# Moving the score visits of an attention and mixer kernel to a schedule that repeats with the batch

## The chip, the cores and the metric

The kernel runs on one core of one Trainium2 chip. A core has five engines that run their own instruction streams: TensorE (PE) for matrix products, VectorE (DVE), ScalarE (ACT), GpSimd (POOL) and SyncE (SP); the last two mostly issue DMAs here. Matrix products go to PSUM, which the program uses as eight banks, and VectorE or ScalarE carry the results from there to SBUF. The metric is the device time of one execution in microseconds, the median of several runs.

## The reference

Eight batches, eight heads, 576 tokens, head width 64. Attention with a causal mask over the tokens, in front of which 16 beacon keys and values stand that every token sees:

```python
k_all = np.concatenate([beacon_k, k], axis=2)
v_all = np.concatenate([beacon_v, v], axis=2)
scores = scale * np.matmul(q, k_all.transpose(0, 1, 3, 2))
causal[:, Nb:] = np.triu(np.ones((S, S), dtype=bool), k=1)
scores = np.where(causal, -1000000000.0, scores)
a = np.exp(scores - scores.max(-1, keepdims=True))
a /= a.sum(-1, keepdims=True) + 1e-09
x = np.matmul(a, v_all)              # heads side by side: (8, 576, 512)
```

Then a mixer: a low-rank product along the tokens (rank 32) with a residual, and two layers of width 2048 with a residual:

```python
h = x.transpose(0, 2, 1) @ U @ V
u = x + h.transpose(0, 2, 1)
out = u + np.maximum(u @ w_ch1, 0.0) @ w_ch2
```

## The kernel before, in words

**Attention in pairs.** The work goes by pairs of heads, p = 0 to 31, four pairs a batch. The score matrix of a pair (keys down, queries across, the causal half only) is cut into four groups of columns, 0 to 3, 496, 464, 496 and 208 wide; each group takes one PSUM bank for each of the two heads. `visit(parts)` (L370) computes the scores of some groups: it takes all its banks, issues the matmuls (L379) for both heads in turn, and then one exponential a bank on ScalarE (L385), which writes to one of four tiles `expt`. `masks_of(p)` (L722) lets VectorE put the masked entries of both heads to zero (L321, L323). `av_of(p)` (L725) gives two units, one a head: 15 matmuls (L394) of the weights with the values, then a reciprocal and a multiply on VectorE (L402, L403) that write into `xb`, the batch's attention output x.

**The mixer.** `mix_units` (L415) gives four steps for a batch once x is there. `turn` (L420) issues five DMA transposes on SP's queue, which write x turned into `uT`. `head` (L426) multiplies x with U: 20 small matmuls and a copy on VectorE. `most` (L449) multiplies with V: it takes four banks, one matmul each (L456), and VectorE adds each to `uT` (L443). `end` (L463) does the last 80 tokens in one bank (L469, L443). 

**The layers.** `mlp_units` (L515) cuts each block of 512 tokens into 32 layer units of four 512-wide matmuls: 16 of the first layer (L531, each with a bank and an eviction into `gT` by ScalarE, L544, or VectorE, L546) and 16 of the second, four to a bank (L557); after the fourth VectorE adds the residual (L570) and SP writes the block out (L576). They stand in `queue`; `fill(n)` issues the next n of them between other work. All orders on all engines are written by hand: the program's order is the order of each engine's stream.

**Banks.** `pst` (L105) takes the bank that was given back longest ago, and `emptying` gives one back in program order when its eviction is issued. So a matmul into a bank waits for the eviction of whatever had it before, and how far back that lies is set by the order of the program alone.

**The stage of the change.** From pair 16 on (`P6`, batches 4 to 7), keys and queries come ready turned by DMA (`turns`, L647: ten transposes a batch on SP's queue, issued at the start of the batch before), and scores are computed in visits of three groups, six banks. 15 pairs with four groups make 20 visits. `long_slot` (L953) is one pair's slot, and its form goes by `r = (p - P6) % 3`: in three slots four visits, whose groups cross from one pair to the next. A batch has four slots, so the visits fall elsewhere in each batch. `mix_between` (L928) runs in a batch's last slot, after the second value product: it issues `turn`, and leaves `head`, `most` and `end` in `mixing`. `head` follows the next visit of a slot with r = 0. `between_visits` (L948) issues `most` at the first call by which at least eight layer units (`SINCE`) have gone by, and puts `end` into the queue three places on, where it counts as a unit. Pairs 16 to 31 have queue places for 131 units, four of which hold an `end`.

Of the kernel before, what the change touches and what calls it, by code (L numbers as in the profile page):

```python
# [30 lines left out]
def kernel(  # L31
# [21 lines left out]
    NH2 = H // 2  # L53
# [51 lines left out]
    def pst(shape, dtype, name):  # L105

        b = emptied.pop(0)
        t = psum.tile(shape, dtype, tag=f"bank{b}", name=name)
        bank_of[id(t)] = (b, t)
        return t  # L110

    def emptying(t):
        emptied.append(bank_of.pop(id(t))[0])
# [256 lines left out]
    def visit(parts):  # L370

        at = {p: (p % NH2, qTs[p // NH2], kTs[p // NH2 % 2], expts_of(p)) for p, _ in parts}
        ps = {(p, g, i): pst([P, 512], F32, name=f"sps{i}") for p, g in parts for i in range(2)}
        for p, g in parts:
            c, qT, kT, _ = at[p]
            for ch, qa, w, o in groups[g]:
                for i in range(2):
                    hp = slice(D * i, D * i + D)
                    nc.tensor.matmul(  # L379
                        ps[p, g, i][:, ds(o, w)], kT[hp, c, ds(P * ch, P)], qT[hp, c, ds(qa, w)],  # L380
                        start=True, stop=True,
                    )
        for p, g in parts:
            for i in range(2):
                nc.scalar.activation(  # L385
                    out=at[p][3][i][:, ds(SLOT * g, gw[g])], in_=ps[p, g, i][:, 0 : gw[g]], func=AF.Exp, scale=scale
                )
                emptying(ps[p, g, i])

    def av_unit(b, h, ex, vs, xb):  # L390
        po = pst([P, NT, E], F32, name="po")
        for j in range(NT):
            for c in range(j + 1):
                nc.tensor.matmul(  # L394
                    po[:, j, :],
                    ex[0 : nk[c], ds(blk[(c, j)], P)],
                    vs[0 : nk[c], ds(c * H * E + h * E, E)],
                    start=(c == 0),
                    stop=(c == j),
                )  # L400
        r = rec[:, b * H + h, :, :]
        nc.vector.reciprocal(out=r, in_=po[:, :, D : D + 1])  # L402
        nc.vector.tensor_tensor(  # L403
            out=xb[:, :, ds(h * D, D)], in0=po[:, :, 0:D], in1=r.broadcast_to([P, NT, D]), op=ALU.mult
        )
        emptying(po)
# [216 lines left out]
    NP = B * NH2  # L623
# [3 lines left out]
    def load_batch(b):  # L627
        if b < DT0:
            Ls[b] = qk_tiles()
            emit_loads(b, Ls[b], vss[b % 2])  # L630
        else:
            v_loads(v[b], beacon_v[b], vss[b % 2])

    def load_whole(b):

        Ls[b] = qk_tiles()
        for i, (src, m) in enumerate(((k[b], nk), (q[b], nq))):
            dst = Ls[b][1][i]
            if i == 0:
                beacon_load(nc.gpsimd, beacon_k[b], dst[:, 0, :, :], ALLH)  # L640
            for j in range(NT):
                a = m[j] - nq[j]
                nc.gpsimd.dma_start(  # L643
                    out=dst[a : m[j], j, :, :], in_=src[:, ds(q0[j], nq[j]), :].rearrange("h p d -> p h d")
                )
# [39 lines left out]
    def regroup_of(p):  # L685
        b, c = divmod(p, NH2)
        prs[p] = [regroup(Ls[b][0], c, i, nc.vector.tensor_copy) for i in range(2)]
# [27 lines left out]
    def expts_of(p):  # L715
        return [expts[(2 * p + i) % NE] for i in range(2)]

    def scores_of(p):
        b, c = divmod(p, NH2)
        return score_units(c, qTs[b], kTs[b % 2], expts_of(p), p < NM)  # L720

    def masks_of(p):  # L722
        scores_of(p)[2]()

    def av_of(p):  # L725
        b, c = divmod(p, NH2)
        if c == 0:
            xbs[b] = xbp.tile([P, NT, DM], F16, name="xb", tag="xb")
        return [
            lambda i=i: av_unit(b, 2 * c + i, expts[(2 * p + i) % NE], vss[b % 2], xbs[b]) for i in range(2)  # L730
        ]
# [5 lines left out]

    DT0 = 4
    LAG = 10
    SINCE = 8  # L740
    HINT = 5

    FIRST = [3, 3, 2, 1]
# [4 lines left out]
    queue = []  # L748
    state = {"t": 0}

    def fill_turns(tr, n):
        for u in tr[:n]:
            u()
        del tr[:n]

    def fill(n):
        while n > 0 and queue:
            u = queue.pop(0)
            if u is not None:
                u()  # L760
            n -= 1

    def feed(b):

        while state["t"] < NBLK and 512 * (state["t"] + 1) <= S * (b + 1):
            t = state["t"]
            units, state["part"] = mlp_units(
                512 * t, 512, lambda i, m, t=t: rows[ds(512 * t + P * i, m), :], t % 2, t > 0, t == NBLK - 1
            )
            queue.extend(units)  # L770
            state["t"] += 1
# [18 lines left out]
    with tc.manual_schedule(engines={ENG.PE, ENG.Activation, ENG.DVE, ENG.SP, ENG.Pool}):  # L790
# [42 lines left out]
        for p in range(2):  # L833
# [4 lines left out]
            av = av_of(p)  # L838
# [5 lines left out]
        av = av_of(2)  # L844
# [8 lines left out]
        av = av_of(3)  # L853
# [30 lines left out]
        for p in range(NH2, NP1):  # L884
            b, c = divmod(p, NH2)
# [39 lines left out]
        P6 = DT0 * NH2  # L925
        mixing = []

        def mix_between(b):  # L928

            turn, head, parts = mix_units(xbs[b], S * b)  # L930
            turn()
            mixing[:] = [head] + parts
            state["since"] = 0
            feed(b)

        def go(n):
            fill(n)
            state["since"] += n

        def visit_then_head(parts):  # L940
            parts = [(p, g) for p, g in parts if p < NP]
            if not parts:
                return
            visit(parts)
            if len(mixing) == 3:
                mixing.pop(0)()

        def between_visits():  # L948
            if len(mixing) == 2 and state["since"] >= SINCE:
                mixing.pop(0)()  # L950
                queue.insert(3, mixing.pop(0))

        def long_slot(p, av):  # L953

            r = (p - P6) % 3
            if r == 0:
                visit_then_head([(p + 1, 0), (p + 1, 1), (p + 1, 2)])
            go(2)
            if r and p < NP:
                masks_of(p)  # L960
            between_visits()
            go(3 if r == 2 else 2)
            av[0]()
            go(1)
            av[1]()
            if p % NH2 == NH2 - 1 and p + 1 < NP:
                mix_between(p // NH2)
            go(1)
            if r == 0:
                visit_then_head([(p + 1, 3), (p + 2, 0), (p + 2, 1)])  # L970
            elif r == 1:
                visit_then_head([(p + 1, 2), (p + 1, 3), (p + 2, 0)])
            else:
                visit_then_head([(p + 1, 1), (p + 1, 2), (p + 1, 3)])
                go(2)
                between_visits()
                go(2)
                if p + 1 < NP:
                    masks_of(p + 1)
                go(2)  # L980

        for p in range(NP1, NP):
            b, c = divmod(p, NH2)
            if c == (1 if p >= P6 else 0) and b + 1 < B:
                load_batch(b + 1)
            if c == 2 and DT0 <= b + 2 < B:
                load_whole(b + 2)
            if c == 0 and b + 1 == DT0:
                tr = turns(b + 1)
            if c == 0 and DT0 < b + 1 < B:  # L990
                tr = turns(b + 1)
            sc = scores_of(p + 1) if p < P6 else []
            qk = qkT_of(p + 2) if p + 2 < min(NP, DT0 * NH2) else []
            av = av_of(p) if p < P6 else []
            if c == 0 and b + 1 == DT0:
                fill_turns(tr, NT)
            if c == 0 and b > NF and p <= P6:
                (mix if p < P6 else mix_between)(b - 1)
            if c == 1 and b + 1 == DT0:
                fill_turns(tr, NT)  # L1000
            if c == 0 and b + 1 > DT0:
                fill_turns(tr, 2 * NT)
            if p >= P6:
                long_slot(p, av_of(p))
                continue
            seq = sc[0:1] + av[0:1] + qk[0:1] + sc[1:3] + qk[1:2] + av[1:2]
            if p + 3 < min(NP, DT0 * NH2):
                seq.append(lambda p=p: regroup_of(p + 3))
            quota = QUOTA.get(b, 9)
            done = 0  # L1010
            for i, u in enumerate(seq):
                u()
                want = quota * (i + 1) // len(seq)
                fill(want - done)
                done = want
# [59 lines left out]
    with tc.If(n_bad != 0, label="general"):  # L1075
        with tc.For_i(0, B, 1) as bi:
# [10 lines left out]
            _, head, parts = mix_units(xb, 0, False)  # L1087
# [3 lines left out]
            for t0 in range(0, S, 512):  # L1091
                n = min(512, S - t0)
# [32 lines left out]
```

## Time and profile before

| What | Value |
|---|---|
| Time of three runs, median | 359.1 us (358.96 to 359.97) |
| Profiled execution, its own time | 360.71 us |
| Profiled execution, span from first to last instruction | 359.1 us |
| Granted TensorE clock in that execution, mean | 0.999 |
| Stage with six-bank visits (first and last L379) | 131.8 to 269.3 us |
| Score matmuls of that stage (L379) | 180 |
| Products with the values in all (L394) | 960 |

In the lines of the profile, PE is TensorE's matmuls and PEld its weight loads, DVE VectorE, ACT ScalarE, SP and POOL the two that issue DMAs; a q behind the name is the engine's queue. L379 is line 379 of the program. A line of a timeline gives start, duration, engine, source line, operation, what is written and from what, the shape, and how many alike were put together; in brackets the idle time of the engine before it and what ended it. A matmul's duration runs from its issue to its end, and the next one streams meanwhile.

### The profile page before, as it was taken

What the parts mean: (1) busy time and instruction counts of PE and PEld (TensorE: products, weight loads), DVE (VectorE), ACT (ScalarE), POOL (GpSimd) and SP (SyncE); (2) the same over time, 40 slices, a digit from 0 to 9 for tenths busy, and PEclk for the clock granted to TensorE, in tenths of its full rate; (3) what the DMA queues carried; (4) which work ended last, traced back from release to release, by engine and by line L of the source; (5) the groups of instructions that cost most, each with busy time, mean ns of one, the idle gap of its engine ahead of it and who ended that gap; (6) DMA issues with size and microseconds to landing.
All of it is one profiled execution on the core that took longest, in us unless ns stands there. A gap on an engine that the chain in (4) does not pass through costs nothing.

```text
span 359.1 us, 7837 instructions
## 1 busy us (share of the span) xinstructions
PE 349.5 (97%) x3110; PEld 176.1 (49%) x3110; DVE 187.3 (52%) x484; ACT 165.5 (46%) x359; POOL 97.7 (27%) x137
## 2 busy tenths in 40 slices
PE   8999999999999999899999999999999999999995
PEld 3774555455554444445444444454544544444443
DVE  4665874588967644652563545544644634313311
ACT  4976951487733664338523663277225202301400
POOL 8956705327446047202840220000000000000000
PEclk9999999999999999999999999999999999999999
DMA  9999999999999949996999797333013323013111
GB/s 179 97 206 167 154 204 174 210 154 131 103 162 148 172 33 124 149 211 71 133 138 197 118 111 127 108 92 64 32 60 88 58 69 102 16 58 93 26 60 65
DMA packets 146636, 41.89 MB, mean 117 GB/s; under 512 B 131488, under 2 KB 142080, under 8 KB 146592
## 3 DMA queue, kind: packets, MB, share of 16 engines
q0 software_dynamic: 87440, 18.18, 66.2%
q1 hardware_dynamic: 58928, 22.84, 36.3%
q8 instruction: 26, 0.43, 0.5%
q10 hardware_dynamic: 224, 0.30, 0.3%
q14 instruction: 18, 0.15, 0.2%
HBM read 37.37 MB, written 9.44 MB: 130 GB/s over the span
## 4 chain that ended last, share of the span: by engine, by line
PE 82%; DMA 7%; DVE 5%; SPq 2%; ACT 1%; issue 1%; DVEq 0%
PE gps L531 32%; PE cps L557 29%; PE po L394 7%; DMA uT<-xb 5%; PE sps L345 4%; SPq L422 2%; PE sps L379 2%; DVE uT L443 2%; PE tps L274 2%; DMA kT<-st 1%; PE tps L280 1%; PE cph L583 1%; ACT expt L351 1%; DMA stq<-in_q_dram 1%; DVE xb L403 1%
## 5 line engine op out<-in xcount | busy, mean ns | idle before, releaser
L531 PE MATMUL gps<-uT,w 128*128 128x512 f16 x576 | 135.2, 380 | 0.1
L557 PE MATMUL cps<-w,gT 128*128 128x512 f16 x560 | 130.8, 380 | 0.3 <-DVE xb L403 0.3
L544 ACT ACTIVATE gT<-gps 128x512 f16<-128x512 f32 x86 | 52.1, 614 | 83.8 <-PE gps L531 81.9
L557 PEld LDWEIGHTS <-gT 128*128 128x128 f16 x560 | 50.8, 98 | 60.6 <-issue 5.4
L531 PEld LDWEIGHTS <-w 128*128 128x128 f16 x576 | 52.0, 98 | 57.9 <-issue 2.1
L385 ACT ACTIVATE expt<-sps 128x496 f16<-128x496 f32 (+2 forms) x120 | 51.5, 535 | 52.0 <-PE sps L379 52.0
L351 ACT ACTIVATE expt<-sps 128x496 f16<-128x496 f32 (+2 forms) x136 | 58.8, 556 | 21.6 <-PE sps L345 21.5
L546 DVE TENSOR_SCALAR gT<-gps 128x512 f16<-128x512 f32 x58 | 39.9, 690 | 47.6 <-PE gps L531 46.6
L570 DVE TENSOR_TENSOR ob<-cps,ut 128x512 f32<-128x512 f32 x31 | 21.4, 690 | 47.0 <-PE cps L557 46.5
L217 POOL DMA_DIRECT2D vs<-in_v_dram x50 | 39.8, 810 | 18.4 <-DMA st<-in_beacon_k_dram 5.2
L394 PEld LDWEIGHTS <-expt 128*128 128x128 f16 (+1 forms) x960 | 36.1, 98 | 14.5 <-issue 2.2
L394 PE MATMUL po<-vs,expt 128*128 128x65 f16 (+1 forms) x960 | 39.4, 194 | 0.3 <-DVE expt L321 0.3
L403 DVE TENSOR_TENSOR xb<-po,rec 128x320 f16<-128x320 f32 x64 | 31.5, 491 | 2.2
L402 DVE RECIPROCAL rec<-po 128x5 f32<-128x5 f32 x64 | 12.0, 188 | 27.8 <-PE po L394 27.7
L321 DVE TENSOR_TENSOR expt<-expt,bigmask 128x512 f16<-128x512 f16 x54 | 22.5, 416 | 5.8 <-ACT expt L385 3.4
L199 POOL DMA_DIRECT2D vs<-in_beacon_v_dram x8 | 4.3, 540 | 63.8 <-PE po L394 63.7
L443 DVE TENSOR_TENSOR uT<-ups,uT 128x496 f16<-128x496 f32 x24 | 14.5, 667 | 10.8 <-DMA uT<-xb 4.3
L379 PE MATMUL sps<-qT,kT 64*128 64x80 f16 (+2 forms) x180 | 17.1, 281 | 2.5 <-DVE ob L570 0.8
L345 PE MATMUL sps<-qT,kT 64*128 64x496 f16 (+3 forms) x204 | 18.8, 287 | 0.6 <-DVE qT L307 0.3
L643 POOL DMA_DIRECT2D st<-in_q_dram x20 | 16.9, 865 | 4.8 <-DMA vs<-in_v_dram 2.6
L643 POOL DMA_DIRECT2D st<-in_k_dram x20 | 16.9, 874 | 1.4 <-DMA vs<-in_v_dram 1.4
L307 DVE COPY qT<-tps 128x576 f16<-128x576 f16 (+1 forms) x16 | 11.8, 736 | 5.4 <-PE tps L274 3.2
(95 smaller groups left out, 169.0 us busy)
## 6 DMA issues: line engine op xcount, KB each, us to landing
out_dram<-ob SPq DMA_DIRECT2D x35, 256.0 KB, 2.4
vs<-in_v_dram POOLq DMA_DIRECT2D x18, 128.0 KB, 7.7
w<-in_moe_w_ch_dram POOLq DMA_DIRECT2D x4, 512.0 KB, 6.1
w<-in_moe_w_ch_dram POOLq DMA_DIRECT2D x2, 1024.0 KB, 13.6
st<-in_k_dram POOLq DMA_DIRECT2D x12, 128.0 KB, 7.7
st<-in_q_dram POOLq DMA_DIRECT2D x12, 128.0 KB, 9.8
st<-in_k_dram POOLq DMA_DIRECT2D x2, 576.0 KB, 13.3
st<-in_q_dram POOLq DMA_DIRECT2D x2, 576.0 KB, 15.7
```

Source lines behind the costliest of these rows:

```text
L217: nc.gpsimd.dma_start(out=dst[a : a + nq[j], j, :, :], in_=src[hs, ds(q0[j], nq[j]), :].rearrange("h p d -> p h d"))
L345: nc.tensor.matmul(ps[g, i][:, ds(o, w)], kT[hp, c, ds(P * ch, P)], qT[hp, c, ds(qa, w)], start=not early, stop=True, skip_group_check=early,)
L351: nc.scalar.activation(out=ex[i][:, ds(SLOT * g, gw[g])], in_=ps[g, i][:, 0 : gw[g]], func=AF.Exp, scale=scale)
L379: nc.tensor.matmul(ps[p, g, i][:, ds(o, w)], kT[hp, c, ds(P * ch, P)], qT[hp, c, ds(qa, w)], start=True, stop=True,)
L385: nc.scalar.activation(out=at[p][3][i][:, ds(SLOT * g, gw[g])], in_=ps[p, g, i][:, 0 : gw[g]], func=AF.Exp, scale=scale)
L394: nc.tensor.matmul(po[:, j, :], ex[0 : nk[c], ds(blk[(c, j)], P)], vs[0 : nk[c], ds(c * H * E + h * E, E)], start=(c == 0), stop=(c == j),)
L403: nc.vector.tensor_tensor(out=xb[:, :, ds(h * D, D)], in0=po[:, :, 0:D], in1=r.broadcast_to([P, NT, D]), op=ALU.mult)
L531: nc.tensor.matmul(g[:, 0:n], w1[:, cc, ts(dc, P)], uT[:, cc, ds(t0, n)], start=(cc == 0), stop=(cc == NCC - 1))
L544: nc.scalar.activation(out=gT["t"][:, dc, 0:n], in_=g[:, 0:n], func=AF.Relu)
L546: nc.vector.tensor_scalar_max(out=gT["t"][:, dc, 0:n], in0=g[:, 0:n], scalar1=0.0)
L557: nc.tensor.matmul(ps[:m, :], gT["t"][:, dc, ds(P * i, m)], w2[:, dc, :], start=(dc == 0), stop=turned and dc == NDC - 1, skip_group_check ...
L643: nc.gpsimd.dma_start(out=dst[a : m[j], j, :, :], in_=src[:, ds(q0[j], nq[j]), :].rearrange("h p d -> p h d"))
```

## The change

`SINCE`, `between_visits` and the counting of units go. `go(parts, mixed)` now does a visit and the next `mixed` steps of the mixer at once behind it, and `weighted(av, *n)` the two value products with n layer units behind each. A slot's form goes by its place c in the batch, so that all batches are alike: visits of six banks at the start and the end of slot 0, at the start and the end of slot 2 and in the middle of slot 3, and one of two banks in slot 1. `head` follows the first visit of slot 0; `most` follows the visit of two banks in slot 1 directly, 13 layer units after x is complete; `end` comes three layer units later as a step of its own, and three more end the slot. A batch has 5 + 11 + 6 + 10 = 32 layer units, as many as one block of 512 tokens, and there are 23 visits in all, the last of them of four banks. Between the masks and the first value product of a pair stand 1 layer unit in slot 1, 2 in slot 2 and 4 with a visit among them in slot 3; those of slot 0's pair are issued in slot 3 of the batch before.

```diff
-    SINCE = 8
...
             mixing[:] = [head] + parts
-            state["since"] = 0
             feed(b)
 
-        def go(n):
-            fill(n)
-            state["since"] += n
-
-        def visit_then_head(parts):
+        def go(parts, mixed=0):
+
             parts = [(p, g) for p, g in parts if p < NP]
-            if not parts:
-                return
-            visit(parts)
-            if len(mixing) == 3:
-                mixing.pop(0)()
-
-        def between_visits():
-            if len(mixing) == 2 and state["since"] >= SINCE:
-                mixing.pop(0)()
-                queue.insert(3, mixing.pop(0))
-
-        def long_slot(p, av):
-
-            r = (p - P6) % 3
-            if r == 0:
-                visit_then_head([(p + 1, 0), (p + 1, 1), (p + 1, 2)])
-            go(2)
-            if r and p < NP:
+            if parts:
+                visit(parts)
+            for u in mixing[:mixed]:
+                u()
+            del mixing[:mixed]
+
+        def masks_if(p):
+            if p < NP:
                 masks_of(p)
-            between_visits()
-            go(3 if r == 2 else 2)
-            av[0]()
-            go(1)
-            av[1]()
-            if p % NH2 == NH2 - 1 and p + 1 < NP:
-                mix_between(p // NH2)
-            go(1)
-            if r == 0:
-                visit_then_head([(p + 1, 3), (p + 2, 0), (p + 2, 1)])
-            elif r == 1:
-                visit_then_head([(p + 1, 2), (p + 1, 3), (p + 2, 0)])
+
+        def weighted(av, *n):
+            for u, m in zip(av, n):
+                u()
+                fill(m)
+
+        def long_slot(p, c, av):
+
+            if c == 0:
+                go([(p + 1, 0), (p + 1, 1), (p + 1, 2)], 1)
+                fill(2)
+                weighted(av, 1, 2)
+                go([(p + 1, 3), (p + 2, 0), (p + 2, 1)])
+            elif c == 1:
+                fill(2)
+                masks_of(p)
+                fill(1)
+                weighted(av, 1, 1)
+                go([(p + 1, 2)], 1)
+                fill(3)
+                go([], 1)
+                fill(3)
+            elif c == 2:
+                go([(p, 3), (p + 1, 0), (p + 1, 1)])
+                fill(2)
+                masks_of(p)
+                fill(2)
+                weighted(av, 1, 1)
+                go([(p + 1, 2), (p + 1, 3), (p + 2, 0)])
             else:
-                visit_then_head([(p + 1, 1), (p + 1, 2), (p + 1, 3)])
-                go(2)
-                between_visits()
-                go(2)
+                fill(2)
+                masks_of(p)
+                fill(3)
+                go([(p + 1, 1), (p + 1, 2), (p + 1, 3)])
+                fill(1)
+                weighted(av, 1, 0)
                 if p + 1 < NP:
-                    masks_of(p + 1)
-                go(2)
+                    mix_between(p // NH2)
+                fill(2)
+                masks_if(p + 1)
+                fill(1)
...
-                long_slot(p, av_of(p))
+                long_slot(p, c, av_of(p))
```

## The prediction

> **What bounds the kernel now.** I read the page first, then the busy time in stretches, then TensorE's timeline, and last the timelines of the engines it waits for.
>
> ```profile
> span 359.1 us, 7837 instructions
> PE 349.5 (97%) x3110; PEld 176.1 (49%) x3110; DVE 187.3 (52%) x484; ACT 165.5 (46%) x359; POOL 97.7 (27%) x137
> ...
> L531 PE MATMUL gps<-uT,w 128*128 128x512 f16 x576 | 135.2, 380 | 0.1
> ```
>
> TensorE (PE) is the bound; the other engines are near half. So the change can only gain where TensorE stands still. The stretches around four visits of the stage 131 to 270 us, in sum:
>
> ```profile
> sum 12.20, PE 9.41 PEld 3.95 DVE 11.45 ACT 8.00 POOL 3.04; mean PE 2.35 PEld 0.99 DVE 2.86 ACT 2.00 POOL 0.76
> ```
>
> These are 144 to 149, 183 to 186, 218 to 221 and 253.9 to 255.1: 12.20 - 9.41 = 2.79 us idle. That is too little, because a matmul's row holds its whole passage (380 ns above) while the next is already streaming. What counts is the time from the start of one piece of work to the start of the next:
>
> ```profile
> 131.78 0.79 PE L379 MATMUL sps<-qT,kT 64*128 64x496 f16 x10
> 132.50 0.47 PE L431 MATMUL qtp<-xb,Usb 112*32 112x128 f16 x20
> 132.90 2.76 PE L531 MATMUL gps<-uT,w 128*128 128x512 f16 x12
> ...
> 138.15 1.03 PE L557 MATMUL cps<-w,gT 128*128 128x512 f16 x4
> 139.11 0.67 PE L379 MATMUL sps<-qT,kT 64*128 64x208 f16 x6
> 139.71 1.90 PE L557 MATMUL cps<-w,gT 128*128 128x512 f16 x8
> 141.54 0.39 PE L456 MATMUL ups<-Vsb,qts 32*128 32x496 f16 x4
> 141.86 1.90 PE L557 MATMUL cps<-w,gT 128*128 128x512 f16 x8
> ...
> 145.38 0.31 PE L469 MATMUL uend<-Vend,qts 128*128 128x80 f16 x4
> 145.62 0.43 PE L379 MATMUL sps<-qT,kT 64*128 64x336 f16 x6
> ...
> 148.69 4.49 PE L557 MATMUL cps<-w,gT 128*128 128x512 f16 x20 [0.26 <-DVE xb L403]
> 153.01 0.62 PE L394 MATMUL po<-vs,expt 128*128 128x65 f16 x15
> 153.47 1.03 PE L557 MATMUL cps<-w,gT 128*128 128x512 f16 x4
> ...
> 155.75 0.68 PE L379 MATMUL sps<-qT,kT 64*128 64x464 f16 x10
> 156.36 1.04 PE L557 MATMUL cps<-w,gT 128*128 128x512 f16 x4
> ...
> 175.79 0.69 PE L379 MATMUL sps<-qT,kT 64*128 64x336 f16 x10
> 176.41 1.90 PE L557 MATMUL cps<-w,gT 128*128 128x512 f16 x8
> ...
> 183.35 0.63 PE L379 MATMUL sps<-qT,kT 64*128 64x464 f16 x3
> ...
> 185.48 5.35 PE L557 MATMUL cps<-w,gT 128*128 128x512 f16 x24
> ...
> 218.19 1.03 PE L379 MATMUL sps<-qT,kT 64*128 64x496 f16 x4
> ...
> 220.35 3.63 PE L557 MATMUL cps<-w,gT 128*128 128x512 f16 x16
> ...
> 253.98 1.10 PE L379 MATMUL sps<-qT,kT 64*128 64x208 f16 x6
> ...
> 255.02 3.63 PE L557 MATMUL cps<-w,gT 128*128 128x512 f16 x16
> ```
>
> Prices from these starts. A layer unit is four 512-wide matmuls: 153.01 - 148.69 = 4.32 for five, so 0.865. A value product of one head (L394): 153.47 - 153.01 = 0.46. The head (L431): 132.90 - 132.50 = 0.40. The products with V of the low-rank mixer (L456, "most"): 0.32. The end (L469): 0.24. A visit of six banks that isn't blocked: 0.72 (131.78, groups 0 1 2), 0.60 (139.11, groups 3 0 1), 0.61 (155.75, groups 1 2 3), 0.62 (175.79, groups 2 3 0). Entering a visit from a layer unit costs 0.10 more (139.11 - 138.15 = 0.96 against 0.865), and so does entering most (141.54 - 139.71 = 1.83 for two units).
>
> Against these stand the four blocked visits: 145.62 to 148.69 is 3.07 where 0.62 is the price (2.45 lost), 183.35 to 185.48 is 2.13 for 0.61 (1.52), 218.19 to 220.35 is 2.16 for 0.72 (1.44), 253.98 to 255.02 is 1.04 for 0.60 (0.44). Sum 5.85 us. Each is the first visit after most and end, with at most three or four layer units in between: it needs six of the eight PSUM banks, and they come free in the order of their last use, so it gets the four of most and the one of end, which VectorE has not emptied.
>
> [...] By the busy share, which the page warns of, the gain would be 2.79 at most, and by starts it is 5.85; I take the second and keep the first as a rival.
>
> **The change part by part.** All matmuls, exponentials and masks stay, as do the orders of the SP and POOL queues; what moves is where the visits, most, end and the masks stand among 128 layer units. I call a batch's six visits A, B (slot 0), T (the one of two banks), C, D (slot 2) and E (slot 3). The order on TensorE is A head 5 units with 2 products, B 5 with 2, T most 3 end 3, C 6 with 2, D 5, E 5 with 2.
>
> *The block after most.* C comes three units, end and three units after most. VectorE's part:
>
> ```profile
> 140.78 0.69 DVE L570 TENSOR_TENSOR ob<-cps,ut 128x512 f32<-128x512 f32 x1 [1.72 <-PE cps L557]
> 141.39 0.41 DVE L321 TENSOR_TENSOR expt<-expt,bigmask 128x512 f16<-128x512 f16 x1
> 141.72 0.19 DVE L323 TENSOR_TENSOR expt<-expt,mask 80x80 f16<-80x80 f16 x1
> ...
> 144.36 2.42 DVE L443 TENSOR_TENSOR uT<-ups,uT 128x496 f16<-128x496 f32 x4 [2.01 <-PE po L394]
> ...
> 148.55 0.48 DVE L443 TENSOR_TENSOR uT<-uend,uT 128x320 f16<-128x320 f32 x1
> ```
>
> Four banks of most take VectorE 2.42 us, one output eviction 0.6 from start to start (141.39 - 140.78), end 0.48. From the start of most to C are 0.32 + 3 x 0.865 + 0.24 + 3 x 0.865 + 0.10 = 5.85 us. VectorE begins about 0.4 after most's start and has most at 2.8, the eviction at 3.4, end (multiplied at 3.2) at 4.0. C waits for nothing, 1.8 us to spare: all 5.85 us lost before come back. What hid the transposed x before was nothing (VectorE sat until 144.36); now it must land before most:
>
> From the chain of waits, issue to landing, and SP's timeline:
>
> ```profile
> 134.99 9.15 DMA uT<-xb
> ```
>
> ```profile
> 131.03 6.62 SPq L422 DMA_TRANSPOSE uT<-xb  x5
> ```
>
> The five x transposes begin on SP's queue at 131.03, and the fourth, the last that most's sums need, lands at 134.99 + 9.15 = 144.14. A starts at 131.78 as before. From A to most: A 0.72, head 0.40, five units 4.32, two products 0.92, 0.10, B 0.60, five units 4.32, two products 0.92, 0.10, T about 0.3, that is 12.7, so 144.5 or later. It is covered with 0.4 us and VectorE's wait is gone; without that cover the 1.8 us before C go first. In later batches three units (2.6) lie between the last product and A, so there is more room.
>
> *The masks of slot 1.* Here the change adds a wait. After B come two units, the masks of this pair, one unit, then its first product; before, two units lay between masks and product. The second unit after B is the fourth quarter of an output block (A is followed by its first two), so its eviction stands ahead of the masks on VectorE, which works in the order of the program. From B's start: 0.60, two units to 2.33, eviction starts 0.2 later (140.78 against a unit ending at 139.71 + 0.865 = 140.58), mask 0.61 after that at 3.14, its first instruction ends at 3.55. The third unit ends at 3.20. So TensorE waits 0.35 and for the semaphore and the weight load behind it; with 0.15 for these (the 0.2 of the eviction is the nearest row) it is 0.5, in each of four batches: 2.0 us. Bounds: 1.4 (no such latency) and 2.4 (the product also waits for L323, which ends at 141.91, 0.1 after L321). Behind the waiting product stands all of TensorE's work, so the wait counts in full; behind the mask on VectorE are only the second head's mask and these products' divisions, which aren't late. The exponentials are no part of it:
>
> ```profile
> L385 ACT ACTIVATE expt<-sps 128x208 f16<-128x208 f32 x30 | 8.9, 363 | 12.5 <-PE sps L379 12.5
> ```
>
> The two that this pair lacks (208 wide, 363 ns) come first in B and are done 1.0 after its start.
>
> [...]
>
> *Three more visits.* 23 instead of 20, since five of six banks and one of two carry 16 groups. Each has a fixed part: 0.60 less 1,168 columns at 0.216 / 512 per column (0.49) is 0.11, and 0.10 to enter, so 3 x 0.21 = 0.63. Against that most follows T directly and doesn't pay its own entry, 4 x 0.10. The trace shows no visit of two banks; bounds 0 and 0.65, I take 0.25.
>
> *Close visits.* ScalarE's timeline:
>
> ```profile
> 164.97 2.14 ACT L544 ACTIVATE gT<-gps 128x512 f16<-128x512 f32 x4
> ...
> 204.98 2.48 ACT L385 ACTIVATE expt<-sps 128x496 f16<-128x496 f32 x6 [1.11 <-PE sps L379]
> ```
>
> D and E are 0.62 + 5 x 0.865 + 0.10 = 5.05 us apart. ScalarE has D's six exponentials (2.48, row 204.98) and up to four layer evictions (2.14 together, row 164.97) in that time: 4.62. It fits; E takes three banks of D and those of the first three units, all emptied. Cost 0, and 0.5 each in three batches if it doesn't fit.
>
> *Keys and queries.* D now needs group 0 of the next batch, first in the batch of 131.78. SP's timeline, and that one transpose by itself:
>
> ```profile
> 149.87 1.25 SPq L655 DMA_TRANSPOSE qT<-st  x1
> ...
> DMA to landing us min/median/max: 8.2/8.2/8.2
> ```
>
> The last piece of qT for it is issued at 149.87 and lands 8.2 later, at 158.1. By the prices above most starts at 144.5 + 0.5 (slot 1), C 5.85 later at 150.85, D 0.60 + 6 x 0.865 + 0.92 + 0.10 later at 157.65, and its third group 0.4 on, at 158.05. I take 0.1, bounds 0 and 1.0.
>
> *The tail.* End is now followed by one layer unit, not two, before the last block reads its sum (0.48 on VectorE, 0.4 after its start, behind 0.24 + 0.865): 0.1, bounds 0 and 0.3.
>
> *Sum:* -5.85 + 2.0 + 0.25 + 0.1 + 0.1 = -3.4. The profiled execution took 360.71 us with a span of 359.1; it would take 357.3. The median of the runs was 359.1, and 359.1 - 3.4 = 355.7 is the forecast.
>
> **The rivals.**
> 1. *The mask comes in time* (the product waits for none of it): 355.7 - 2.0 = 353.7. For it: before, no product of this stage waited for a mask. Against: there were two units between then.
> 2. *The keys are late*: D is held up by 1.0 in the two batches whose transposes run beside loads: 355.7 + 2 x 1.0 - 0.1 = 357.6. For it: the margin is nil. Against: the landing times were measured under the same loads.
> 3. *The busy share was right*: only 2.79 come back, less 2.45 of costs: 358.8. Against: the starts above.
> 4. *The block moves to C*: x lands 3 us later than in the trace, which is 0.85 more than the 0.4 and 1.8 us of cover, VectorE holds most's banks, and C stands for 0.85 in each of four batches: 355.7 + 3.4 = 359.1. For it: VectorE did wait for x at 144.36. Against: 3 us is a third of a landing time.
> 5. *Slower.* ScalarE doesn't keep up where visits are five units apart: E (three times) is blocked in its fourth to sixth bank, at the mean of the four blocks, 1.46, so 355.7 + 4.4 = 360.1. It decides once the exponentials of D and four evictions take over 5.05 us. For it: 4.62 of 5.05 is 91%. Against: E takes banks whose evictions come first in that list.
>
> **How the numbers follow.** Forecast 0.58, rivals in order 0.12, 0.08, 0.06, 0.04 and 0.12. Three in a thousand (1.1 us) is what can be told from no change. Faster: 0.58 + 0.12 + 0.08 = 0.78; within: 0.06 + 0.04 = 0.10; slower 0.12. The range reaches from 353.3 (rival 1 with the smallest visit and tail costs) to 358.7 (the upper bounds of masks, visits, keys and tail together, 355.7 + 0.4 + 0.4 + 1.9 + 0.2 = 358.6, and the edge of rival 3).
>
> **What would show it.** On TensorE's timeline the visit after most and end takes 0.60, not 1 to 3 us; VectorE starts most's sums without a wait for uT<-xb; L394 shows four waits for VectorE's L321, some 0.5 each, and their absence is rival 1; a wait of L379 for kT or qT is rival 2; one for ScalarE's L544 or L385 is rival 5. The forecast is wrong if a new gap of over 1 us stands in every batch that isn't named here.

## The result, and the profile after

The kernel after takes 356.38 us, the median of 4 runs (355.61 to 356.55). The kernel before, run beside it, takes 359.03 (358.57 to 359.97). The ratio is 0.9919, with a 95% interval of 0.9894 to 0.9943: 2.65 us less, where 3.4 were forecast, and inside the range of 353.3 to 358.7. One run of before among those beside e9 and e10 in the table below took 501.07 us at a granted clock of 0.658, where all others show 0.992 or more; it is left out of the medians and ratios.

The head of the page of the kernel after:

```profile
span 354.7 us, 7839 instructions
PE 346.1 (98%) x3110; PEld 174.2 (49%) x3110; DVE 188.1 (53%) x484; ACT 165.5 (47%) x359; POOL 97.5 (27%) x137
```

The work of each engine is what it was; the span is 4.4 shorter. That is more than the medians differ by, and not all of it belongs to the change: the first six-bank visit, up to which both programs are alike, starts at 130.54 here and at 131.78 in the profiled execution of before, which was 1.6 above the median of its runs. So I compare from the start of the first six-bank visit to the start of the first output matmul of the last block (L583), and call this the stage. All that the change moves lies in it. The six visits of a batch have the letters of the prediction, A to E and T. TensorE's timeline of before ends the stage with this row:

```profile
351.14 3.66 PE L583 MATMUL cph<-w,gT 128*128 128x256 f16 x32
```

Its stage is 351.14 - 131.78 = 219.36 us. TensorE's timeline of the kernel after:

```profile
130.54 0.79 PE L379 MATMUL sps<-qT,kT 64*128 64x496 f16 x10
...
137.61 2.76 PE L557 MATMUL cps<-w,gT 128*128 128x512 f16 x12
140.63 0.63 PE L394 MATMUL po<-vs,expt 128*128 128x65 f16 x15 [0.25 <-DVE expt L321]
...
143.38 0.39 PE L379 MATMUL sps<-qT,kT 64*128 64x336 f16 x6
143.70 0.39 PE L456 MATMUL ups<-Vsb,qts 32*128 32x496 f16 x4
...
149.45 0.67 PE L379 MATMUL sps<-qT,kT 64*128 64x208 f16 x6
150.05 2.76 PE L557 MATMUL cps<-w,gT 128*128 128x512 f16 x12
...
156.25 0.48 PE L379 MATMUL sps<-qT,kT 64*128 64x336 f16 x8
157.75 0.39 PE L379 MATMUL sps<-qT,kT 64*128 64x496 f16 x2 [1.02 <-DMA qT<-st]
158.07 4.49 PE L531 MATMUL gps<-uT,w 128*128 128x512 f16 x20
162.49 0.67 PE L379 MATMUL sps<-qT,kT 64*128 64x464 f16 x10
163.09 1.04 PE L531 MATMUL gps<-uT,w 128*128 128x512 f16 x4
...
194.15 0.69 PE L379 MATMUL sps<-qT,kT 64*128 64x336 f16 x10
194.77 4.49 PE L531 MATMUL gps<-uT,w 128*128 128x512 f16 x20
...
347.01 3.66 PE L583 MATMUL cph<-w,gT 128*128 128x256 f16 x32
```

The stage is now 347.01 - 130.54 = 216.47, 2.89 less. C, the visit after most and end, goes from 149.45 to 150.05: 0.60, its price when nothing blocks it. What is new are two waits, and TensorE's table of waits between 130 and 270 us (engine, line and what it waited for; us in total, times, longest) has no others:

```profile
PE sps L379 <- DMA qT<-st: 1.0, 1, 1.0
PE po L394 <- DVE expt L321: 1.0, 4, 0.3
```

By starts, each mask wait costs 0.43: three layer units from 137.61 would end at 137.61 + 3 x 0.865 = 140.20, and the product starts at 140.63. The key wait, in D of the first batch, costs 158.07 - 156.25 = 1.82 less 0.62, that is 1.20. So the stage should change by -5.85 + 4 x 0.43 + 1.20 = -2.93, and it changed by -2.89.

VectorE's timeline around the first most:

```profile
139.55 0.69 DVE L570 TENSOR_TENSOR ob<-cps,ut 128x512 f32<-128x512 f32 x1 [3.44 <-PE cps L557]
140.16 0.41 DVE L321 TENSOR_TENSOR expt<-expt,bigmask 128x512 f16<-128x512 f16 x1
...
144.12 2.42 DVE L443 TENSOR_TENSOR uT<-ups,uT 128x496 f16<-128x496 f32 x4 [0.78 <-PE ups L456]
...
147.05 0.48 DVE L443 TENSOR_TENSOR uT<-uend,uT 128x320 f16<-128x320 f32 x1
```

Most's sums begin 0.42 after most (143.70), and now wait for TensorE and not for the transposed x; the end's is done at 147.53, two microseconds before C. The mask at 140.16 stands behind the eviction at 139.55, as the sum had it.

### The profile page after: what moved, and what is told of

It is laid out like the page before. It is cut to its first block, busy times and chain, and to the rows that moved or that the text cites. A ratio compares the mean times of both kernels' runs of the same rounds, so it can differ in the third digit from the quotient of the medians.

```text
span 354.7 us, 7839 instructions
## 1 busy us (share of the span) xinstructions
PE 346.1 (98%) x3110; PEld 174.2 (49%) x3110; DVE 188.1 (53%) x484; ACT 165.5 (47%) x359; POOL 97.5 (27%) x137
## 4 chain that ended last, share of the span: by engine, by line
PE 86%; DMA 5%; DVE 2%; ACT 2%; issue 1%; SPq 1%; POOL 1%; POOLq 0%; DVEq 0%
PE gps L531 33%; PE cps L557 30%; PE po L394 8%; PE sps L345 4%; PE sps L379 3%; DMA st<-in_k_dram 3%; DMA qT<-st 2%; PE tps L274 2%; ACT expt L351 2%; SPq L655 1%; PE idle L249 1%; PE cph L583 1%; PE tps L280 1%; PE qtp L431 1%; POOL vs L217 1%
## 5 line engine op out<-in xcount | busy, mean ns | idle before, releaser
L531 PE MATMUL gps<-uT,w 128*128 128x512 f16 x576 | 136.8, 379 | 0.1
L570 DVE TENSOR_TENSOR ob<-cps,ut 128x512 f32<-128x512 f32 x31 | 21.4, 690 | 54.1 <-PE cps L557 53.9
L394 PEld LDWEIGHTS <-expt 128*128 128x128 f16 (+1 forms) x960 | 35.8, 98 | 16.6 <-DVE expt L321 3.8
L394 PE MATMUL po<-vs,expt 128*128 128x65 f16 (+1 forms) x960 | 39.5, 194 | 1.3 <-DVE expt L321 1.3
L379 PE MATMUL sps<-qT,kT 64*128 64x80 f16 (+2 forms) x180 | 14.8, 281 | 1.0 <-DMA qT<-st 1.0
```

What stands on the lines that cost most here:

```text
L379: nc.tensor.matmul(ps[p, g, i][:, ds(o, w)], kT[hp, c, ds(P * ch, P)], qT[hp, c, ds(qa, w)], start=True, stop=True,)
L394: nc.tensor.matmul(po[:, j, :], ex[0 : nk[c], ds(blk[(c, j)], P)], vs[0 : nk[c], ds(c * H * E + h * E, E)], start=(c == 0), stop=(c == j),)
L531: nc.tensor.matmul(g[:, 0:n], w1[:, cc, ts(dc, P)], uT[:, cc, ds(t0, n)], start=(cc == 0), stop=(cc == NCC - 1))
```

## The experiments

Two theories stand to be told apart. Mine was that the blocks before came from the nearness of the visit to most and end together with the lateness of x, and that the new placing of the visits cures them at the price of two waits. The rival is that the 13 layer units between x and most do it alone, and the regrouping of the visits gains nothing by itself. All results first; e1 to e4 share one set of runs of before, e5 to e8 another on the same chip, e9 and e10 a third on another chip. The stage is taken from TensorE's timeline of each profiled execution, from the first L379 to the first L583.

| Kernel | Median us | Before beside it | Ratio, 95% interval | Stage us |
|---|---|---|---|---|
| before | 359.03 | | | 131.78 to 351.14: 219.36 |
| after | 356.38 | 359.03 | 0.9919 [0.9894, 0.9943] | 130.54 to 347.01: 216.47 |
| e1_masks_early | 354.73 | 357.80 | 0.9920 [0.9894, 0.9946] | 130.20 to 345.28: 215.08 |
| e2_keys_first | 355.03 | 357.80 | 0.9919 [0.9897, 0.9942] | 130.65 to 345.92: 215.27 |
| e3_both | 353.49 | 357.80 | 0.9875 [0.9845, 0.9904] | 130.62 to 344.17: 213.55 |
| e4_lag13_alone | 354.74 | 357.80 | 0.9919 [0.9894, 0.9944] | 130.11 to 344.75: 214.64 |
| e5_after_again | 355.92 | 359.71 | 0.9922 [0.9891, 0.9953] | 130.30 to 345.99: 215.69 |
| e6_late_x_far_visit | 355.39 | 359.71 | 0.9898 [0.9862, 0.9935] | 130.26 to 345.69: 215.43 |
| e7_near_visit_x_in_time | 355.62 | 359.71 | 0.9903 [0.9866, 0.9940] | 130.39 to 345.69: 215.30 |
| e8_lag13_end5_keys | 353.83 | 359.71 | 0.9846 [0.9819, 0.9874] | 130.32 to 344.88: 214.56 |
| e9_both_again | 353.33 | 358.14 | 0.9855 [0.9828, 0.9882] | 130.42 to 343.96: 213.54 |
| e10_lag13_queries_first | 353.60 | 358.14 | 0.9865 [0.9838, 0.9893] | 130.39 to 343.82: 213.43 |

The median of before is 357.80 to 359.71 by the chip and the set of runs, a spread as large as the effects looked for here; therefore the readings below go by the stage and by single visits, and the ratios stand beside them. The stage of before is known from one execution only. That execution spent 360.71 - 219.36 = 141.35 us outside the stage, the others 139.5 to 140.3. By these, the medians of before leave 217.5 to 220.2 for its stage, which is an estimate. So a gain against before's 219.36 can be too large by up to 1.9 us, while the other versions are compared among themselves, each by its own stage.

**The masks one unit earlier** (on the kernel after, slot 1):

```diff
-                fill(2)
+                fill(1)
                 masks_of(p)
-                fill(1)
+                fill(2)
```

> The changed kernel with slot 1's masks issued after one layer unit instead of two, so ahead of the output eviction on VectorE. Theory (the mask waits behind that eviction): the four waits of 0.43 us of L394 for L321 go, but D of the first batch comes 0.43 sooner and waits that much longer for qT, so about 1.3 us less than the changed kernel's 356.4: 355.1, and 355.9 on a kernel before of 360. Rival (the product waits for its exponentials, or the wait goes elsewhere on VectorE): no difference, 356.4.

TensorE's timeline of this kernel:

```profile
137.27 2.76 PE L557 MATMUL cps<-w,gT 128*128 128x512 f16 x12
139.87 0.61 PE L394 MATMUL po<-vs,expt 128*128 128x65 f16 x15
...
155.48 0.48 PE L379 MATMUL sps<-qT,kT 64*128 64x336 f16 x8
157.31 0.39 PE L379 MATMUL sps<-qT,kT 64*128 64x496 f16 x2 [1.35 <-DMA qT<-st]
157.63 1.68 PE L531 MATMUL gps<-uT,w 128*128 128x512 f16 x7
```

The product now starts 2.60 after the start of the three units, their bare price, with no wait. But D comes 0.43 earlier, counted from the first six-bank visit (25.28 and 25.71), and its third group only 0.10 (27.11 and 27.21): its wait is 157.63 - 155.48 - 0.62 = 1.53, 0.33 more than in the kernel after. The stage is shorter by 1.39 = 4 x 0.43 - 0.33. So the four mask waits cost 1.72 in all, and part of what they give up is lost again to the next thing that is late.

The two traces show what the order on VectorE does: with the eviction (139.55) ahead of the mask (140.16) the product waits 0.43, with the mask ahead (137.35, the eviction at 139.21) it does not wait.

**The keys and queries of group 0 first** (on the kernel after, in `turns`; both kinds of the early columns go before those of the late ones):

```diff
+        if b > DT0:
+            us = [us[i] for i in (0, 1, 3, 5, 7, 2, 4, 6, 8, 9)]
         return us
```

> The changed kernel with the ten transposes of keys and queries in another order: those that group 0 of the next batch reads (kT 0, qT 0 to 3) first. They are then the first five instead of the first eight, some 4 us sooner. Theory (D waits for the eighth transpose in the first batch, 1.2 us): that wait goes, 355.2. Rival (the landing is set by the loads beside it, not by the place on SP's queue): the wait stays, 356.4.

TensorE's timeline, D of the first batch:

```profile
156.36 0.69 PE L379 MATMUL sps<-qT,kT 64*128 64x336 f16 x10
156.97 3.19 PE L531 MATMUL gps<-uT,w 128*128 128x512 f16 x14
```

D takes 0.61 and its wait is gone. The stage is 1.20 shorter than after's, as much as the wait cost there.

**Both edits together**, in two sets of runs:

> Both edits together. Theory: no wait of TensorE is left between 130 and 270 us; 4 x 0.43 + 1.2 = 2.9 us less than the changed kernel: 353.5. Rival (one wait only gives way to the next, a bank or a key): 355 or more.

> The changed kernel with both edits (masks after one unit, keys of group 0 first) once more, beside the next. 353 to 354.5; stage from the first visit to L583 213.5 us, no wait of TensorE in it.

The stage is 213.55 and 213.54, 2.92 below after's: 1.72 + 1.20. No wait of TensorE is left in the table of waits of that stretch. Against before it is 5.81 shorter, so nearly the whole 5.85 that the starts had shown as lost has come back.

**The lag alone.** The kernel before with its own grouping of the visits, and only the number of units between x and most changed:

```diff
-    SINCE = 8
+    SINCE = 13
```

> The kernel before with one number changed: most is issued at the first call with 13 layer units behind x instead of 8; visits, masks and units stand as before. Theory (most of the 5.85 us came from VectorE waiting for the turned x while it held most's four banks): what remains are visits close behind end with x in time, at the price of the fourth block, 0.44, or 0.8 where only three units and end lie between, some 1.8 us in all: 4 us less than before, 355.0. Rival (the nearness of visit and end is what blocks, whenever x lands, so that the visits have to be regrouped): three or four blocks of 1 to 2 us stay, 358 to 359.

The stage is 214.64, 4.72 shorter than before's and 1.05 to 1.83 shorter than in the two executions of the kernel after (e5, after). By the ratio to before the two kernels can't be told apart (0.9919 each), and by the medians this one gains 3.06 against the 357.80 beside it.

No sum of most waits for x in this kernel, and the visits are as near to most as they were. From the start of most to the visit after it are 4.08, 5.11, 3.16 and 4.09 us in the four batches of before, and 4.94, 3.16, 4.07 and 4.08 here. Two visits of before meet their like here, with the same steps between most and visit and, by the program's order, the same six banks. The second one of before loses 1.52 with x late (most stands at 178.24, the fourth transpose of x, issued at 172.6, lands 8.4 later, at 181.0, and most's sums begin at 181.21); its like (151.63, in the first batch) takes 0.61. The third loses 1.44; its like, directly behind the end of 184.71, is the first of these on TensorE's timeline, and the second is the visit of the third batch:

```profile
184.95 0.79 PE L379 MATMUL sps<-qT,kT 64*128 64x496 f16 x10
185.67 2.76 PE L557 MATMUL cps<-w,gT 128*128 128x512 f16 x12
...
219.74 1.10 PE L379 MATMUL sps<-qT,kT 64*128 64x208 f16 x6
220.77 2.55 PE L557 MATMUL cps<-w,gT 128*128 128x512 f16 x11
```

The first takes 0.72, unblocked. The second takes 1.03 for 0.60. A visit in the fourth batch loses 0.43 as well, and the visit at 191.87 in the second batch loses some 0.45 to a wait for a piece of qT: 1.3 together, and 214.64 - 213.43 = 1.21 is what this kernel lacks to the best one with this grouping (e10). On VectorE's timeline most's sums of the second batch wait for TensorE alone; the last three rows show what the blocked visit of the third batch stands behind:

```profile
182.20 2.42 DVE L443 TENSOR_TENSOR uT<-ups,uT 128x496 f16<-128x496 f32 x4 [2.06 <-PE ups L456]
...
216.38 2.41 DVE L443 TENSOR_TENSOR uT<-ups,uT 128x496 f16<-128x496 f32 x4
...
219.93 0.49 DVE L403 TENSOR_TENSOR xb<-po,rec 128x320 f16<-128x320 f32 x1
220.34 0.48 DVE L443 TENSOR_TENSOR uT<-uend,uT 128x320 f16<-128x320 f32 x1
```

Most's banks were emptied at 218.79, a microsecond before the visit. The end's sum is done at 220.82, after the layer unit behind the visit has begun (220.77), so it isn't the end's bank that the visit waits for. It is that of the value product just ahead, whose division is done at 220.42; by the program's order it is the visit's sixth bank. The fourth block of before, 0.44, is of this kind. VectorE's timeline of before, in the third and then in the fourth batch:

```profile
216.97 2.42 DVE L443 TENSOR_TENSOR uT<-ups,uT 128x496 f16<-128x496 f32 x4 [4.29 <-DMA uT<-xb]
...
250.60 2.41 DVE L443 TENSOR_TENSOR uT<-ups,uT 128x496 f16<-128x496 f32 x4
...
254.17 0.49 DVE L403 TENSOR_TENSOR xb<-po,rec 128x320 f16<-128x320 f32 x1
254.58 0.48 DVE L443 TENSOR_TENSOR uT<-uend,uT 128x320 f16<-128x320 f32 x1
```

In the fourth batch x was not late, since the sums at 250.60 wait for nothing. The division ends at 254.66, the end's sum at 255.06, and the unit behind the visit begins at 255.02.

**The kernel after once more**, unchanged, to see how firm its waits are:

> The changed kernel once more, as the measure for the other three of this set. 355.5 to 356.5; from the first six-bank visit to the last half block (L583) 216.5 us, as in its first profile.

TensorE's timeline, D of the first batch:

```profile
156.01 0.48 PE L379 MATMUL sps<-qT,kT 64*128 64x336 f16 x8
...
157.03 3.20 PE L531 MATMUL gps<-uT,w 128*128 128x512 f16 x14
```

The four mask waits are the same, 1.0 in all in the table of waits. D takes 1.02, 0.40 over its price, where the first execution had 1.20, and the stage is 0.78 shorter. The transpose that D waited for in the first execution was issued 18.01 us after the first visit there (148.55) and 17.6 after it in this one (147.9), and landed 8.9 and 8.5 later:

```profile
DMA to landing us min/median/max: 8.9/8.9/8.9
```

```profile
DMA to landing us min/median/max: 8.5/8.5/8.5
```

So the landing came 0.8 sooner, and D took 0.80 less. This trace puts the idle time ahead of D's third group (0.23, ended at 156.72) down to TensorE's own L379 and not to the transpose; that it is the key wait is read from the landing, at 156.4. Between these two executions that wait is the one term that differs; what it was in the other runs behind the medians (0.9919 and 0.9922 of before), no trace shows.

**x late, the visit far.** On the kernel after, the visit of two banks and most go three units and two products' places forward within slot 1, so that most comes 10 units behind x, while C stands nine units and two products behind most:

```diff
-                fill(2)
+                fill(1)
                 masks_of(p)
                 fill(1)
-                weighted(av, 1, 1)
                 go([(p + 1, 2)], 1)
+                fill(1)
+                weighted(av, 1, 1)
```

> The changed kernel with slot 1's masks after one unit (as in the run of that edit alone, which took 1.39 us less in the stage), and the visit of two banks with most brought forward ahead of the value products, to ten units behind x. Most then comes some 2.7 us before the turned x lands in the first of these batches, 1.4 in the second; but six units, two products, end and three units lie between most and visit C, 9.4 us. Theory (it takes both, x late and the next visit near, to stop TensorE): VectorE waits and TensorE doesn't; the time is that of the masks' edit alone, 1.4 less than the changed kernel. Rival (x landing after most costs by itself, through what is queued behind on VectorE): 2 us or more above that.

VectorE's timeline, and TensorE's:

```profile
143.26 2.42 DVE L443 TENSOR_TENSOR uT<-ups,uT 128x496 f16<-128x496 f32 x4 [3.30 <-DMA uT<-xb]
```

```profile
148.73 0.67 PE L379 MATMUL sps<-qT,kT 64*128 64x208 f16 x6
149.33 2.76 PE L557 MATMUL cps<-w,gT 128*128 128x512 f16 x12
```

VectorE stands 3.30 us for x, where it stood 2.01 in this batch before the change (there x landed at 144.14, 0.22 ahead of the sums, though the row names L394), and C is not blocked: 0.60. (In the second batch it stands 0.59; in the others x is in time.) The masks are early here, as in e1, and so the stage is to be held against e1's: 215.43 against 215.08. TensorE's table of waits has only the one for the queries, 1.7 where e1 has 1.4; by starts that wait costs 1.88 against 1.53, which is the whole 0.35. A late x by itself costs nothing.

**x in time, the visit near.** On the kernel after, C goes right behind the end:

```diff
                 go([], 1)
-                fill(3)
             elif c == 2:
                 go([(p, 3), (p + 1, 0), (p + 1, 1)])
-                fill(2)
+                fill(5)
```

> The changed kernel with visit C right behind end, and the three units between moved behind C. x is in time; most to C is 0.32 + 2.6 + 0.24 = 3.2 us instead of 5.85. Theory: VectorE has end's bank, the sixth that C takes, at 3.9, so C is blocked for 0.4 in each of four batches: 1.6 us above the changed kernel. Rival (with x in time nearness costs nothing): no difference.

TensorE's timeline:

```profile
146.47 0.31 PE L469 MATMUL uend<-Vend,qts 128*128 128x80 f16 x4
146.71 0.68 PE L379 MATMUL sps<-qT,kT 64*128 64x208 f16 x6
147.31 5.35 PE L557 MATMUL cps<-w,gT 128*128 128x512 f16 x24
...
156.10 0.69 PE L379 MATMUL sps<-qT,kT 64*128 64x336 f16 x10
156.72 3.63 PE L531 MATMUL gps<-uT,w 128*128 128x512 f16 x16
```

C takes 0.60 directly behind the end, as it does far from it. The expectation had the end's bank as its sixth. By the order of the banks it takes the second of T, the four of most and one of an output block, neither the end's nor a value product's, so this run doesn't repeat the blocks left in e4; of most's banks it shows that a near visit finds them empty when x is in time: their sums (143.96, 2.42 long) are done at 146.38, and C starts at 146.71. The stage is 0.39 shorter than e5's, because here D happens not to wait (0.62). One order of the transposes has now shown 1.20, 0.40 and 0.

**The old grouping with the lag, the end later, and the keys reordered.** On the kernel before:

```diff
-    SINCE = 8
+    SINCE = 13
...
-                queue.insert(3, mixing.pop(0))
+                queue.insert(5, mixing.pop(0))
...
+        if b > DT0:
+            us = [us[i] for i in (0, 1, 3, 5, 7, 2, 4, 6, 8, 9)]
         return us
```

> The kernel before with most 13 units behind x, end five units behind most instead of three, and the keys that group 0 reads turned first: no regrouping of the visits. Theory (the visits need no regrouping): the two blocks of 0.4 and the wait of 0.4 for qT that the lag alone left go, though in the first batch a layer unit now reads end's sum at once and may wait 0.6: 0.6 to 1.2 less than with the lag alone, 3.0 below the changed kernel in the stage at best. Rival (blocks come back elsewhere): as much as the lag alone.

TensorE's timeline, the visit of groups 3, 0 and 1 in the second batch:

```profile
192.24 0.47 PE L379 MATMUL sps<-qT,kT 64*128 64x208 f16 x4
193.61 0.37 PE L379 MATMUL sps<-qT,kT 64*128 64x464 f16 x2 [0.89 <-DMA qT<-st]
193.91 1.25 PE L531 MATMUL gps<-uT,w 128*128 128x512 f16 x5
```

No visit stands for a bank any more. With end behind the visit, the visit gets the first value product's bank as its sixth and not the second's, and a layer unit stands in end's place. But this visit needs the other end of qT, which that order turns last: 193.91 - 192.24 - 0.60 = 1.07 lost. Hence the same with the last piece of the queries moved up, `(0, 1, 3, 5, 7, 9, 2, 4, 6, 8)`:

> The kernel before with most 13 units behind x, end five units behind most, and kT 0 and all five pieces of qT turned first, since its visit of groups 3, 0 and 1 also reads the last piece of qT, which landed last in the run before. Theory: the wait of 0.9 for qT goes, and the old grouping of the visits is as good as the new one with both edits: stage 213.6 us, time within 0.5 of the run beside it. Rival (the grouping that repeats with the batch is worth something by itself): 1 us or more above the run beside it.

The same visit on TensorE's timeline:

```profile
192.25 0.67 PE L379 MATMUL sps<-qT,kT 64*128 64x208 f16 x6
192.84 2.33 PE L531 MATMUL gps<-uT,w 128*128 128x512 f16 x10
```

The visit takes 0.59, the table of waits of the stage is empty, and the stage is 213.43: 5.93 below before, and 0.12 from that of the regrouped kernel with its two waits removed (e3, e9). The medians on one chip, 353.60 and 353.33, differ by 0.27 the other way. So neither grouping is worth more than some 0.3 us by itself, where the rival asked for 1. By the stage these are the best versions of this study; both beat the kernel before and the kernel after.

## Why the prediction was right

**The blocked visits, -5.85.** Right in size and in the rows that were to show it: C takes 0.60, VectorE no longer waits for x. With every new wait removed, 5.81 (e3) and 5.93 (e10) come back against the profiled execution of before. By the medians of e3, e8, e9 and e10 it is 4.3 to 5.9, so an average run of before may have lost less than 5.85.

**Their cause.** The prediction named the nearness of the visit to most and end, and the late x as what delayed VectorE. The runs say that the large blocks need both: late and near (the first three blocks of before) loses 5.41, late and far (e6) nothing, in time and far (after) nothing, in time and near nothing (e7, and the first two visits of e4). The fourth block, 0.44, has another cause, as have the two of 0.43 in e4: the visit takes the bank of the value product just ahead of the end. To remove the lateness alone (e4) is worth 4.72 by the stage and 3.06 by the medians. What the prediction took for the gain of the new schedule is for the most part the gain of five more units between x and most, which it holds as well; the pattern that repeats with the batch is not needed for it.

On the banks the prediction was wrong. It gave a blocked visit the four of most and the one of end. By the program's order the visits of before take three or four of most, the others of value products, output blocks and an earlier visit, and end's in the second only. The one that came free last was an output's in the first and the third (L570, done at 148.00 and 219.99), end's in the second (185.25), and the second value product's in the fourth. In the first three it made no difference to the sum, because all of these stand behind most's sums on VectorE and were late with them.

**The masks, 2.0 within 1.4 to 2.4.** Right: 4 x 0.43 = 1.72, shown by e1. The sum had 0.35 for the mask and 0.15 for what lies behind it. By the rows the mask ends at 140.57, 0.37 after the units, and the product starts 0.06 behind it.

**Three more visits 0.25, the tail 0.1.** The tail cost nothing: from the end to the layer unit after next, 295.01 - 294.01 = 1.00, is its 0.14 and one unit. For the visits there is only the remainder, -2.89 + 2.93 = 0.04, at the low end of 0 to 0.65; T itself took 143.70 - 143.38 = 0.32, as the prediction had it. No run took the extra visits alone, but both groupings without any wait (e9 and e10) differ by 0.11 in the stage, so the three visits, less whatever else the regrouping saves, cost about that.

**Keys and queries, 0.1 within 0 and 1.0.** This is the term that was mis-sized: it cost 1.20 in the profiled execution and 0.40 in the next, above its upper bound in the first. Counted from the first visit, the piece landed at 26.91 (148.55 + 8.9) where the prediction had 26.29, from one row of 8.2; D's third group would have started at 26.01 (156.25 + 0.30) and not at 26.27; and TensorE went on 0.30 after the landing, where the prediction let the wait end with it. With the 0.02 that it had, 0.02 + 0.62 + 0.26 + 0.30 = 1.20. A margin of nil was given the price of a margin, as if one landing had no spread.

**The sum.** By the first profiled execution it is -5.85 + 1.72 + 1.20 + 0.04 = -2.89 against -3.4. The difference of 0.5 is 1.1 more for the keys, and 0.28, 0.21 and 0.1 less for masks, visits and tail. The medians differ by 2.65.

**The rivals.** The mask did not come in time (0.43 in each batch). The keys were late, in part: in the first batch only, while D of the second (194.15 to 194.77) takes 0.62. The busy share was wrong: it gave 2.79 as the most that could come back, and e10 got 5.93 by the stage and 4.54 by the medians without any change in the work. A layer matmul's row is 380 ns long on average and the next one starts after 216 (4.32 us for twenty); the new waits show the same in small, 0.25 idle in the row and 0.43 by starts. The block did not move to C (0.60). ScalarE kept up: E, 163.09 - 162.49, takes 0.60.

## What to carry to other kernels

Price a stall by the distance from start to start against the same work unblocked, and then ask for every condition it needs: here the visit had to be near and its bank's eviction late, and to remove the second one took a change of one number. Work out from the program's order which bank the stalled work takes, and hold the end of its eviction against the start of the work: that told the end's bank from the value product's. Where a new order leaves a transfer no margin, give its lateness the spread of several landings, not the one that a single trace shows. And when a wait is removed, look at once for what is late next: the masks gave back 1.39 of 1.72 until the keys were moved too.

## What the runs showed of the hardware

The same DMA transpose, at the same place of the same program, landed 8.9 and 8.5 us after its issue in two executions, and 8.2 in the kernel before. In the second of the two executions it was also issued some 0.4 us sooner on SP's queue, and the visit behind it lost 0.40 there, 1.20 in the first. TensorE went on some 0.3 us after the landing (157.45 and 157.75 in the kernel after, 156.4 and 156.72 in e5). VectorE stood for 3.30 us at the head of its queue without any cost to TensorE (e6): the end's sum was done at 147.92, before C started at 148.73.
